# A list scheduler's table of priority offsets: 170 groups of operations in place of 21

## The chip, the cores and the metric

One core of one Trainium2 chip runs the whole program. The metric is device time in microseconds (us) of one execution; lower is better. Engines go by their names in the profile: PE is TensorE's matmul, PEld its weight load, DVE is VectorE, ACT is ScalarE, POOL is GpSimd, SP is SyncE, which issues all the DMAs here.

## The reference

Attention over 8 batches x 8 heads with queries averaged in pairs, and behind it a feed-forward block (FFN) whose gate is a cosine:

```python
q_pool = q.reshape(B, H, S // 2, 2, D).mean(axis=3)          # S 1152, D 64
scores = scale * q_pool @ k.transpose(0, 1, 3, 2)
attn = exp(scores - max(scores)); attn = attn / (sum(attn) + 1e-09)
x = (attn @ v).transpose(0, 2, 1, 3).reshape(B * S // 2, H * D)   # 4608 x 512
h = x @ w_in                                                   # 512 x 2048
out = (h * cos(h)) @ w_out                                     # 2048 x 512
```

All inputs and the output are f32; q and k have a spread of 0.8.

## The kernel before

To keep f32 accuracy with f16 matmuls, nearly each operand is split into a high and a low f16 part (cast on ACT, difference on POOL or DVE), and products are made as high x high, high x low, low x high.

Attention goes over 32 pairs of heads, each in 9 units. For a pair n, long before its units begin: K and q are loaded (SP), cast and split (`prep_k`, L745 and L746; `prep_q1`, L762; `prep_q2`, L775), and transposed by DMA into `k1`, `q1T`. PE makes trial scores into the banks `mx` (named m at L815, `mx_main`), DVE reduces them to row maxima `mxs` (L826), the maxima are negated into a column of `qs2`, which is transposed into `q2T`. In a unit: PE makes scores into two `st` banks (L1265; the rest rows L1286), ACT makes the exponent `e` (L1315) and its f16 cast `pp` (L1323), POOL or DVE the low part of `pp` (L1329, L1325), and PE multiplies with `vc`, V scaled, into the sums `ava` and `avb` (L1355; the mixed rows L1400), one PSUM bank each. For the first three pairs, and partly for the next ones, e is used as f32 (`NF32`, forms f32 of L1355 and L1400). At a pair's end `av_end` empties the two banks through DVE (L1454, L1459, L1462, L1469) into `xp`, of which there are two.

FFN goes over 18 chunks of 256 rows. A batch's four `xp` are scaled, split (`xs2`, L1523 ACT, L1525 DVE) and transposed to `xT`. `ffn1` multiplies with the two parts of w_in into banks `f` (L1630); ACT evicts each bank twice (L1654, L1657), DVE once (L1658); a sine (L1563), a product (L1569), a cast and a split (L1580, L1581) give the gate `g`; `ffn2` multiplies with w_out (L1690), DVE scales (L1734) and SP stores. The weights arrive as 64-bit floats: 16 pieces of 1 MB go through `big` buffers, DVE decodes each in three steps (L568, L571, L574; output named w for w_in and wf for w_out) and takes maxima (L585; for w_in ACT does, L581), ACT scales and casts (L608, L609), POOL splits (L612). w1 is ready when the last scale of w_in is there (L652 runs then). Until there is an FFN group to run, PE has attention alone. Sixty small warm-up matmuls (L663) stand between 14 and 26 us.

The order of the instructions on each engine is not that of the code. The code emits all instructions once; `arrange` then makes a list of 8,337 entries (one for each instruction of DVE, ACT, POOL and SP, one for a run of matmuls into one tile on PE), finds what depends on what, and schedules the list with estimated costs: each engine, when it comes free, takes of the entries that are ready the one with the smallest key. A key is the entry's place in the code's order plus an offset. The result is then fixed: each engine runs its instructions strictly in that order, with the usual semaphore waits. The offset comes from the table `SHIFT`, looked up by engine, operation, tiles written and tiles read:

```python
if nd["ins"][0].name in fill:
    off += len(nodes)
elif group in SHIFT:
    off += SHIFT[group][k * 1 // len(nodes)]
nd["key"] = (k + off, k)
```

A negative offset lets a group go ahead of others that are ready at the same time, a positive one lets it stand back. Tiles in the table go by the tag of their buffer: mx is the trial scores' banks, f those of FFN, `big` the large buffers (raw weights, FFN's h and y), `w2_1` also the place where w_in is decoded, `w2_0` that where pair 1's q and k lie at first.

Of the kernel before, what the change touches and what calls it, by code (L numbers as in the profile page):

```python
# [62 lines left out]
HS = (-16, -15, -14, -13, -12, -10, -12, -11, -10, -9, -8, -7, -7)  # L63

SHIFT = {
    ("Activation", "Activati", "big", "big"): (20,),
    ("Activation", "Activati", "big", "big/wsc"): (80,),
    ("Activation", "Activati", "vc_0", "sv/vld"): (20,),
    ("Activation", "TensorCo", "pp", "e"): (-80,),
    ("DVE", "TensorRe", "wmx", "big"): (-20,),  # L70
    ("DVE", "TensorSc", "big", "big/f/r1a"): (-40,),
    ("DVE", "TensorSc", "vc_1", "sv/vc_1/vld"): (80,),
    ("DVE", "TensorTe", "big", "big"): (20,),
    ("DVE", "TensorTe", "xp", "ava/rs"): (-300,),
    ("DVE", "TensorTe", "xp", "avb/rs"): (-40,),
    ("PE", "Matmult", "avb", "g/w2_0/w2_1"): (20,),
    ("PE", "Matmult", "avb", "w1_0/w1_1/xT"): (-20,),
    ("PE", "Matmult", "mx", "k1_0/q1T"): (-150,),
    ("PE", "Matmult", "mx", "w1_0/w1_1/xT"): (-40,),
    ("PE", "Matmult", "st", "g/w2_0/w2_1"): (-150,),  # L80
    ("PE", "Matmult", "st", "k1_1/k2_0/q1T/q2T"): (-20,),
    ("Pool", "TensorTe", "w2_1", "big/w2_0"): (-150,),
    ("SP", "DMACopy", "out_0", "xo"): (-150,),
    ("SP", "DmaTrans", "k1_0", "kst"): (-20,),
    ("SP", "DmaTrans", "q1T", "q1s"): (20,),
    ("SP", "DmaTrans", "xT", "xs2"): (150,),
}
# [1882 lines left out]
```

## Time and profile before

| | us |
|---|---|
| median of 3 runs | 1528.41 |
| lowest, highest | 1524.58, 1537.75 |
| the profiled execution's own time | 1523.91 |
| its span, first to last instruction | 1522.1 |
| PE busy in it | 1489.3 (98%) |
| ACT, DVE, POOL busy | 1231.5, 1042.9, 978.7 |

The rows below come from the profiled execution. Its own time is the one to set beside its span; the median of the runs is what a change is measured by. The share of busy time is an average over stretches with different limits, so a row for a stretch says more than one for the whole.

### The profile page before, as it was taken

To read this page: it belongs to the slowest core of one execution; us is meant where nothing else is said; L and a number is where in the kernel's file an instruction comes from. 1 tells how busy PE (TensorE), PEld (TensorE's weight loads), DVE (VectorE), ACT (ScalarE), POOL (GpSimd) and SP (SyncE) were. 2 spreads that over 40 slices of the span, in tenths; PEclk is the share of its full clock that TensorE was granted. 3 is DMA by queue.
4 is the path that set the end of the run, shared out by engine and by line. 5 is a ranking of instruction groups with operands and counts; after the bars stand their busy time and mean duration, and the time that the engine had idled before them with its cause. 6 is when DMAs were issued, how large, how long until landed. Compare 5 with 4: busy or idle time off the path is not lost.

```text
span 1522.1 us, 37816 instructions
## 1 busy us (share of the span) xinstructions
PE 1489.3 (98%) x15569; PEld 1022.5 (67%) x15569; DVE 1042.9 (69%) x1935; ACT 1231.5 (81%) x1925; POOL 978.7 (64%) x852
## 2 busy tenths in 40 slices
PE   6999899999999999999999999999999999999998
PEld 4777677667666576666666667666666667766665
DVE  6998876856786687786747776766777775532332
ACT  5778689998999799997977897998998898944442
POOL 4454567886776868778575676686878677531222
PEclk9999999999999999999999999999999999999999
DMA  9976634534255343535322425345352521001000
GB/s 257 299 211 150 172 82 96 116 76 108 71 102 111 98 91 73 127 68 138 83 73 65 98 63 115 78 99 104 87 108 73 110 56 31 11 27 30 20 17 22
DMA packets 226110, 145.07 MB, mean 95 GB/s; under 512 B 202448, under 2 KB 204752, under 8 KB 223888
## 3 DMA queue, kind: packets, MB, share of 16 engines
q1 hardware_dynamic: 225936, 142.65, 39.8%
q8 instruction: 122, 2.00, 0.5%
q14 instruction: 52, 0.43, 0.1%
HBM read 74.45 MB, written 10.49 MB: 56 GB/s over the span
## 4 chain that ended last, share of the span: by engine, by line
PE 84%; DVE 6%; ACT 5%; DMA 2%; issue 1%; POOL 1%; SPq 0%; ACTq 0%; DVEq 0%; POOLq 0%
PE f L1630 20%; PE f L1690 19%; PE st L1265 14%; PE ava L1355 8%; PE avb L1355 6%; PE m L815 6%; PE st L1286 2%; DVE mxs L826 2%; PE mx L1690 1%; DMA kld<-in_k_dram 1%; ACT e L1315 1%; PE ava L1400 1%; ACT pp L1323 1%; PE st L1630 1%; PE mx L856 1%
## 5 line engine op out<-in xcount | busy, mean ns | idle before, releaser
L1329 POOL TENSOR_TENSOR pp<-e,pp 128x512 f16<-128x512 f32 x438 | 531.0, 1236 | 235.7 <-ACT pp L1323 121.2
L826 DVE TENSOR_REDUCE mxs<-m 128x1 f32<-128x512 f32 x464 | 304.0, 681 | 109.9 <-PE m L815 108.1
L1630 PEld LDWEIGHTS <-w 128*128 128x128 f16 x3456 | 333.2, 98 | 65.6 <-DVE y L1658 2.1
L1630 PE MATMUL f<-xT,w 128*128 128x256 f16 x3048 | 365.6, 273 | 2.1 <-DVE y L1658 2.1
L1315 ACT ACTIVATE e<-st 128x512 f32<-128x512 f32 x534 | 295.8, 604 | 48.6 <-PE st L1265 26.7
L1690 PE MATMUL f<-w,g 128*128 128x512 f16 x1440 | 333.3, 379 | 0.0
L1581 POOL TENSOR_TENSOR g<-hsc,g 128x512 f16<-128x512 f32 x144 | 185.9, 1312 | 172.3 <-ACT g L1580 136.9
L1323 ACT CAST pp<-e 128x1024 f16<-128x1024 f32 x267 | 282.0, 1056 | 4.7 <-PE avb L1355 2.1
L1690 PEld LDWEIGHTS <-g 128*128 128x128 f16 x1680 | 161.1, 98 | 182.5 <-issue 0.7
L1355 PEld LDWEIGHTS <-pp 128*128 128x128 f16 (+1 forms) x5857 | 236.6, 100 | 67.5 <-issue 12.8
L1265 PE MATMUL st<-q1T,k 128*128 128x512 f16 x576 | 218.7, 380 | 2.6 <-ACT pp L1315 1.6
L1265 PE MATMUL st<-q2T,k 128*128 128x512 f16 x576 | 218.7, 380 | 0.0
L1355 PE MATMUL ava<-vc,pp 128*128 128x65 f16 (+6 forms) x4020 | 214.6, 202 | 2.3 <-DVE lx L1485 1.5
L1355 PE MATMUL avb<-vc,pp 128*128 128x65 f16 (+3 forms) x2329 | 176.8, 207 | 0.3 <-POOL pp L1329 0.3
L1265 PEld LDWEIGHTS <-k 128*128 128x128 f16 x1152 | 100.8, 98 | 95.1 <-issue 20.4
L1569 DVE TENSOR_TENSOR hsc<-hsc,y 128x512 f32<-128x512 f32 x144 | 133.8, 962 | 40.4 <-ACT y L1563 40.1
L815 PE MATMUL m<-k,q1T 128*128 128x512 f16 x464 | 154.6, 380 | 4.8 <-DVE mxs L826 4.1
L1658 DVE SCALAR_TENSOR_TENSOR y<-f,r1a,y 128x512 f32<-128x512 f32 x127 | 94.6, 746 | 81.6 <-ACT y L1657 79.4
L1654 ACT ACTIVATE hsc<-f,small 128x512 f32<-128x512 f32 x127 | 88.4, 696 | 62.7 <-PE f L1630 62.3
L1580 ACT CAST g<-hsc 128x512 f16<-128x512 f32 x144 | 88.7, 626 | 30.6 <-PE f L1690 29.6
L1325 DVE TENSOR_TENSOR pp<-e,pp 128x1024 f16<-128x1024 f32 x48 | 84.8, 1767 | 31.1 <-ACT pp L1323 22.8
L746 POOL TENSOR_TENSOR kst<-kld,kst 128x1152 f16<-128x1152 f32 x30 | 72.6, 2420 | 28.6 <-ACT kst L745 18.4
(183 smaller groups left out, 1898.5 us busy)
## 6 DMA issues: line engine op xcount, KB each, us to landing
vld<-in_v_dram SPq DMA_DIRECT2D x32, 576.0 KB, 3.9
...
```

Of the source, the lines that this page charges most:

```text
L815: nc.tensor.matmul(banks[h], q1T[n][:, h * QT + t, :], kmain(n, k1[n % 3], c, h), start=True, stop=True, skip_group_check=True,),
L826: nc.vector.reduce_max(mxs[n][:, h * QT + t, c : c + 1], banks[h], axis=AX.X)
L1265: nc.tensor.matmul(s[y].rearrange("p (t c) -> p t c", c=P), kcol(p, w, j, h), x[:, h * QT : (h + 1) * QT, :], start=part == 0, stop=part == 1,
L1315: nc.scalar.activation(e[:, c], b[:, 0 : c.stop - c.start], AF.Exp, scale=exp_scale, bias=l_add)
L1323: nc.scalar.copy(pp[:, 0, c0:n], e[:, c0:n])
L1329: nc.gpsimd.tensor_sub(pp[:, 1, c], e[:, c], pp[:, 0, c])
L1355: mm = nc.tensor.matmul(out, w, x, start=start, stop=False, skip_group_check=True)
L1569: nc.vector.tensor_mul(hj, hj, y[:, j : j + 2])
L1581: nc.gpsimd.tensor_sub(gt[:, 1], hj, gt[:, 0])
L1630: mm = nc.tensor.matmul(ps[:, fi, :], w1[wt][:, hp, fs], ck.xT[hp][:, xi, cs], start=n == 0, stop=n == 3 * HP - 1, skip_group_check=True,)
L1658: nc.vector.scalar_tensor_tensor(yj, ps, ra, yj.bitcast(I32), ALU.mult, ALU.subtract)
L1690: nc.tensor.matmul(po, gt[:, gi, f % 2, ts_], w2[wt][:, f, :], start=f == 0 and (gi, wt) == (0, 0), stop=f == NF - 1 and (gi, wt) == (1, 0),)
```

## The change

Only the table `SHIFT` is changed. It had 21 groups with offsets between -300 and 150; it has 170 groups now, of the 190 that the list has, with offsets between -600 and 600 in steps of 5. Each group of both tables occurs in the kernel. No instruction, tile, buffer or dependency is touched, nor the costs that the scheduler goes by; what changes is the order on the five engines. Lines of groups that the prediction doesn't speak of are left out of the diff.

```diff
 SHIFT = {
-    ("Activation", "Activati", "big", "big"): (20,),
-    ("Activation", "Activati", "big", "big/wsc"): (80,),
-    ("Activation", "TensorCo", "pp", "e"): (-80,),
-    ("DVE", "TensorSc", "big", "big/f/r1a"): (-40,),
-    ("DVE", "TensorTe", "big", "big"): (20,),
-    ("DVE", "TensorTe", "xp", "ava/rs"): (-300,),
-    ("DVE", "TensorTe", "xp", "avb/rs"): (-40,),
-    ("PE", "Matmult", "mx", "k1_0/q1T"): (-150,),
-    ("PE", "Matmult", "st", "k1_1/k2_0/q1T/q2T"): (-20,),
-    ("Pool", "TensorTe", "w2_1", "big/w2_0"): (-150,),
-    ("SP", "DMACopy", "out_0", "xo"): (-150,),
-    ("SP", "DmaTrans", "q1T", "q1s"): (20,),
-    ("SP", "DmaTrans", "xT", "xs2"): (150,),
...
+    ("Activation", "Activati", "big", "big"): (-110,),
+    ("Activation", "Activati", "big", "big/wsc"): (435,),
+    ("Activation", "Activati", "big", "f/r1a"): (-600,),
+    ("Activation", "Activati", "big", "f/small"): (-585,),
...
+    ("Activation", "Activati", "e", "st"): (285,),
...
+    ("Activation", "Activati", "pp", "st"): (-600,),
...
+    ("Activation", "Activati", "w2_1", "w2_1/wsc"): (-290,),
...
+    ("Activation", "TensorCo", "kst", "kld"): (585,),
+    ("Activation", "TensorCo", "pp", "e"): (-340,),
...
+    ("Activation", "TensorCo", "q1s", "qld"): (430,),
...
+    ("Activation", "TensorCo", "w1_0", "w2_1"): (-600,),
+    ("Activation", "TensorCo", "w2_0", "big"): (-170,),
...
+    ("DVE", "TensorRe", "mxs", "f"): (145,),
+    ("DVE", "TensorRe", "mxs", "mx"): (180,),
+    ("DVE", "TensorRe", "mxs", "st"): (-215,),
...
+    ("DVE", "TensorRe", "wmx", "big"): (35,),
...
+    ("DVE", "TensorSc", "big", "big"): (520,),
+    ("DVE", "TensorSc", "big", "big/f/r1a"): (185,),
...
+    ("DVE", "TensorSc", "w2_1", "big"): (430,),
+    ("DVE", "TensorSc", "w2_1", "big/w2_1"): (120,),
...
+    ("DVE", "TensorSc", "xs2", "ratio/xp/xs2"): (-600,),
+    ("DVE", "TensorTe", "big", "big"): (235,),
...
+    ("DVE", "TensorTe", "pp", "e/pp"): (380,),
...
+    ("DVE", "TensorTe", "xp", "ava/rs"): (-80,),
+    ("DVE", "TensorTe", "xp", "avb/rs"): (545,),
...
+    ("PE", "Matmult", "f", "ident/wmx"): (-440,),
...
+    ("PE", "Matmult", "mx", "k1_0/q1T"): (-340,),
...
+    ("PE", "Matmult", "mx", "k1_2/k2_0/q1T/q2T"): (-585,),
...
+    ("PE", "Matmult", "st", "k1_1/k2_0/q1T/q2T"): (-420,),
...
+    ("Pool", "TensorTe", "g", "big/g"): (10,),
+    ("Pool", "TensorTe", "kst", "kld/kst"): (-85,),
+    ("Pool", "TensorTe", "pp", "e/pp"): (-215,),
+    ("Pool", "TensorTe", "pp", "pp"): (-600,),
+    ("Pool", "TensorTe", "pps", "es/pps"): (-600,),
...
+    ("Pool", "TensorTe", "qs2", "q1s/qld"): (-375,),
+    ("Pool", "TensorTe", "w1_1", "w1_0/w2_1"): (-185,),
...
+    ("Pool", "TensorTe", "w2_1", "big/w2_0"): (-200,),
+    ("SP", "DMACopy", "big", "in_moe_w_in"): (245,),
+    ("SP", "DMACopy", "big", "in_moe_w_out"): (435,),
...
+    ("SP", "DMACopy", "kld", "in_k"): (-560,),
+    ("SP", "DMACopy", "out_0", "xo"): (365,),
...
+    ("SP", "DmaTrans", "q1T", "q1s"): (65,),
...
 }
```

## Rows read from the trace of the kernel before

**Rows 1.** Page, part 1: each engine's busy time.
```profile
...
PE 1489.3 (98%) x15569; PEld 1022.5 (67%) x15569; DVE 1042.9 (69%) x1935; ACT 1231.5 (81%) x1925; POOL 978.7 (64%) x852
...
```

**Rows 2.** Five stretches from start: columns in the first line.
```profile
...
core 0: us, PE busy (x) PEld busy (x) DVE busy (x) ACT busy (x) POOL busy (x), PEclk, DMA share, GB/s
...
12.00:228.00 216.00, 204.66 (x1887) 154.41 (x1888) 189.68 (x369) 160.03 (x266) 112.52 (x115) 0.99 0.74 193
228.00:1292.00 1064.00, 1058.44 (x11954) 714.24 (x11953) 767.58 (x1431) 951.82 (x1485) 786.87 (x666) 1.00 0.40 90
1292.00:1518.00 226.00, 226.00 (x1731) 153.85 (x1729) 81.02 (x130) 115.04 (x169) 69.11 (x56) 1.00 0.07 21
1518.00:1523.00 5.00, 0.19 (x2) 0.00 (x0) 0.42 (x1) 0.00 (x0) 0.00 (x0) 0.89 0.11 26
...
```

**Rows 3.** All waits of PE, longest first.
```profile
...
PE m L971 <- DMA q1T<-q1s: 12.1, 1, 12.1
PE m L815 <- DVE mxs L826: 4.1, 10, 1.1
...
```

**Rows 4.** Matmul groups from 12 to 228 us.
```profile
...
L1265 PE MATMUL st<-q2T,k 128*128 128x512 f16 x103 | 39.5, 383 | 0.0
...
L1400 PE MATMUL ava<-vc,pp 128*128 128x65 f32 x216 | 26.2, 273 | 0.0
...
L815 PE MATMUL m<-k,q1T 128*128 128x512 f16 x71 | 24.6, 386 | 3.6 <-DVE mxs L826 3.0 <-DVE amx L886 0.4
L1355 PE MATMUL ava<-vc,pp 128*128 128x65 f32 x144 | 18.7, 273 | 0.0
...
L1630 PE MATMUL f<-xT,w 128*128 128x256 f16 x132 | 15.9, 273 | 0.0
L901 PE MATMUL m<-k,q1T 128*128 128x512 f16 x32 | 10.5, 378 | 0.8 <-DVE mxs L916 0.7
...
L1022 PE MATMUL m<-k,q1T 128*128 128x128 f16 x2 | 0.3, 216 | 0.0
```

**Rows 5.** The chain's pieces, packed work: start, us, what.
```profile
...
70.06 1.79 PE ava L1400 x16
...
192.43 1.31 PE f L1630 x12
...
254.06 2.62 PE f L1630 x24
...
269.07 2.59 PE f L1690 x12
...
```

**Rows 6.** DVE groups from 12 to 228 us.
```profile
...
L826 DVE TENSOR_REDUCE mxs<-m 128x1 f32<-128x512 f32 x71 | 46.5, 680 | 12.1 <-PE m L815 12.0
...
L574 DVE SCALAR_TENSOR_TENSOR wf<-wraw,wf 128x1024 uint32<-128x1024 uint32 x8 | 11.1, 1392 | 0.0
L571 DVE SCALAR_TENSOR_TENSOR wf<-wraw,wf 128x1024 uint32<-128x1024 uint32 x8 | 10.7, 1332 | 0.0
...
L585 DVE TENSOR_REDUCE wmx<-wf 128x1 bf16<-128x1024 f32 x8 | 9.6, 1208 | 0.0
...
L568 DVE TENSOR_SCALAR wf<-wraw 128x1024 uint32<-128x1024 uint32 x8 | 6.3, 801 | 0.0
...
```

**Rows 7.** The chain's pieces in the first 15 us.
```profile
...
10.53 1.10 DVE w L568
...
14.14 0.61 DVE mxs L986
...
```

**Rows 8.** DVE's timeline from 118 to 120 us.
```profile
...
119.43 0.15 DVE L652 RECIPROCAL rw<-small 128x1 f32<-128x1 f32 x1
...
```

**Rows 9.** DVE's timeline from 776 to 822 us.
```profile
...
779.68 0.16 DVE L1454 TENSOR_SCALAR rs<-avb 128x4 f32<-128x4 f32 x1
...
818.64 0.41 DVE L1462 TENSOR_TENSOR xp<-avb,rs 128x256 f32<-128x256 f32 x1
...
```

**Rows 10.** The stretch between those two; columns as in rows 2.
```profile
...
784.00:820.00 36.00, 36.00 (x232) 22.01 (x230) 18.14 (x27) 23.71 (x38) 15.28 (x11) 1.00 0.22 56
...
```

More of the change, by code (lines that the diff above doesn't have):

```diff
@@ new lines @@
+    ("DVE", "TensorRe", "small", "p2w"): (395,),
+    ("DVE", "TensorRe", "small", "small"): (530,),
+    ("DVE", "TensorRe", "wmw", "f"): (-450,),
+    ("DVE", "TensorRe", "wmx", "big"): (35,),
+    ("DVE", "TensorSc", "amx", "amx"): (-265,),
+    ("DVE", "TensorSc", "big", "avb/big/r1a"): (-40,),
+    ("DVE", "TensorSc", "big", "big"): (520,),
+    ("DVE", "TensorSc", "big", "big/f/r1a"): (185,),
+    ("DVE", "TensorSc", "big", "big/mx/r1a"): (235,),
+    ("DVE", "TensorSc", "big", "big/r1a/st"): (-255,),
@@ new lines @@
+    ("DVE", "TensorSc", "es", "ava/rs"): (440,),
+    ("DVE", "TensorSc", "p2w", "wmw"): (-205,),
+    ("DVE", "TensorSc", "r1a", "small"): (-200,),
+    ("DVE", "TensorSc", "rs", "ava"): (-235,),
+    ("DVE", "TensorSc", "rs", "avb"): (220,),
+    ("DVE", "TensorSc", "small", "amx"): (-210,),
+    ("DVE", "TensorSc", "small", "fst"): (230,),
+    ("DVE", "TensorSc", "small", "p2w/rw"): (95,),
+    ("DVE", "TensorSc", "sv", "sv"): (130,),
+    ("DVE", "TensorSc", "vc_0", "sv/vc_0/vld"): (415,),
@@ new lines @@
+    ("DVE", "TensorSc", "vc_1", "sv/vc_1/vld"): (-320,),
+    ("DVE", "TensorSc", "w2_1", "big"): (430,),
+    ("DVE", "TensorSc", "w2_1", "big/w2_1"): (120,),
+    ("DVE", "TensorSc", "wmw", "wmw"): (40,),
+    ("DVE", "TensorSc", "xp", "ava/rs/xp"): (20,),
+    ("DVE", "TensorSc", "xp", "avb/rs/xp"): (-50,),
+    ("DVE", "TensorSc", "xs2", "ratio/xo/xs2"): (460,),
+    ("DVE", "TensorSc", "xs2", "ratio/xp/xs2"): (-600,),
+    ("DVE", "TensorTe", "big", "big"): (235,),
+    ("DVE", "TensorTe", "fst", "small"): (100,),
@@ new lines @@
+    ("DVE", "TensorTe", "kst", "kld/kst"): (-80,),
+    ("DVE", "TensorTe", "pp", "e/pp"): (380,),
+    ("DVE", "TensorTe", "qld", "qld"): (130,),
+    ("DVE", "TensorTe", "xo", "ava/osc"): (5,),
+    ("DVE", "TensorTe", "xo", "avb/osc"): (80,),
+    ("DVE", "TensorTe", "xo", "f/osc"): (-280,),
+    ("DVE", "TensorTe", "xo", "mx/osc"): (350,),
+    ("DVE", "TensorTe", "xo", "osc/st"): (560,),
+    ("DVE", "TensorTe", "xp", "ava/rs"): (-80,),
+    ("DVE", "TensorTe", "xp", "avb/rs"): (545,),
+    ("PE", "Matmult", "ava", "g/w2_0/w2_1"): (-5,),
@@ new lines @@
+    ("PE", "Matmult", "ava", "pp/pps/vc_0"): (-370,),
+    ("PE", "Matmult", "ava", "pp/pps/vc_1"): (20,),
+    ("PE", "Matmult", "ava", "pp/vc_0"): (20,),
+    ("PE", "Matmult", "ava", "pps/vc_0"): (-240,),
+    ("PE", "Matmult", "ava", "pps/vc_1"): (-145,),
+    ("PE", "Matmult", "ava", "w1_0/w1_1/xT"): (-65,),
+    ("PE", "Matmult", "ava/mx", "k1_0/pp/pps/q1T/vc"): (595,),
+    ("PE", "Matmult", "ava/mx", "k1_0/pps/q1T/vc_0"): (-20,),
+    ("PE", "Matmult", "ava/mx", "k1_1/pps/q1T/vc_0"): (-35,),
@@ new lines @@
+    ("PE", "Matmult", "ava/mx", "k1_1/pps/q1T/vc_1"): (-240,),
+    ("PE", "Matmult", "ava/mx", "k1_2/pps/q1T/vc_0"): (10,),
+    ("PE", "Matmult", "avb", "g/w2_0/w2_1"): (-20,),
+    ("PE", "Matmult", "avb", "pp/vc_0"): (-10,),
+    ("PE", "Matmult", "avb", "pp/vc_1"): (25,),
+    ("PE", "Matmult", "avb", "w1_0/w1_1/xT"): (-100,),
+    ("PE", "Matmult", "f", "ident/mxa"): (45,),
+    ("PE", "Matmult", "f", "ident/wmx"): (-440,),
+    ("PE", "Matmult", "f", "k1_0/k2_0/q1T/q2T"): (10,),
+    ("PE", "Matmult", "f", "k1_0/k2_1/q1T/q2T"): (300,),
@@ new lines @@
+    ("PE", "Matmult", "f", "k1_0/q1T"): (335,),
+    ("PE", "Matmult", "f", "k1_1/k2_1/q1T/q2T"): (-90,),
+    ("PE", "Matmult", "f", "k1_1/q1T"): (-40,),
+    ("PE", "Matmult", "f", "k1_2/k2_0/q1T/q2T"): (-320,),
+    ("PE", "Matmult", "mx", "g/w2_0/w2_1"): (5,),
+    ("PE", "Matmult", "mx", "ident/mxa"): (-10,),
+    ("PE", "Matmult", "mx", "k1_0/k2_0/q1T/q2T"): (-340,),
+    ("PE", "Matmult", "mx", "k1_0/k2_1/q1T/q2T"): (20,),
+    ("PE", "Matmult", "mx", "k1_0/q1T"): (-340,),
+    ("PE", "Matmult", "mx", "k1_1/k2_0/q1T/q2T"): (-450,),
@@ new lines @@
+    ("PE", "Matmult", "mx", "k1_1/k2_1/q1T/q2T"): (-225,),
+    ("PE", "Matmult", "mx", "k1_1/q1T"): (-55,),
+    ("PE", "Matmult", "mx", "k1_2/k2_0/q1T/q2T"): (-585,),
+    ("PE", "Matmult", "mx", "k1_2/k2_1/q1T/q2T"): (5,),
+    ("PE", "Matmult", "mx", "w1_0/w1_1/xT"): (-65,),
+    ("PE", "Matmult", "st", "g/w2_0/w2_1"): (-40,),
+    ("PE", "Matmult", "st", "k1_0/k2_0/q1T/q2T"): (-5,),
+    ("PE", "Matmult", "st", "k1_0/k2_1/q1T/q2T"): (-25,),
+    ("PE", "Matmult", "st", "k1_0/q1T"): (20,),
@@ new lines @@
+    ("PE", "Matmult", "st", "k1_1/k2_0/q1T/q2T"): (-420,),
+    ("PE", "Matmult", "st", "k1_1/k2_1/q1T/q2T"): (-35,),
+    ("PE", "Matmult", "st", "k1_2/k2_0/q1T/q2T"): (-20,),
+    ("Pool", "Memset", "k2_0", ""): (80,),
+    ("Pool", "Memset", "k2_1", ""): (-325,),
+    ("Pool", "Memset", "q1s", ""): (-410,),
+    ("Pool", "Memset", "qs2", ""): (-30,),
+    ("Pool", "Memset", "vc_0", ""): (535,),
+    ("Pool", "Memset", "vc_1", ""): (295,),
+    ("Pool", "Memset", "w2_0", ""): (70,),
+    ("Pool", "Memset", "xo", ""): (195,),
@@ new lines @@
+    ("SP", "DMACopy", "out_0", "xo"): (365,),
+    ("SP", "DMACopy", "qld", "in_q"): (15,),
+    ("SP", "DMACopy", "vld", "in_v"): (80,),
+    ("SP", "DMACopy", "w2_0", "in_k"): (20,),
+    ("SP", "DMACopy", "w2_0", "in_q"): (115,),
+    ("SP", "DMACopy", "xo", "left"): (430,),
+    ("SP", "DmaTrans", "k1_0", "kst"): (-85,),
+    ("SP", "DmaTrans", "k1_1", "kst"): (115,),
+    ("SP", "DmaTrans", "k1_1", "w2_0"): (215,),
+    ("SP", "DmaTrans", "k1_2", "kst"): (5,),
+    ("SP", "DmaTrans", "q1T", "q1s"): (65,),
@@ L87 @@
+    ("SP", "DmaTrans", "q2T", "qs2"): (10,),
+    ("SP", "DmaTrans", "q2T", "w2_0"): (-535,),
 }
```

49 lines of the change are left out of this document (41 added, 8 removed).

## The prediction

> **What bounds the kernel now.** I read the engines' busy times first, then the same by stretches, then what PE waits for, then the groups and the chain in the one stretch where PE is not full. TensorE (PE) is busy 1489.3 of 1522.1 us, 98%; ScalarE comes next with 81% [rows 1]. The 33 us that PE sits idle lie at few places [rows 2, 3]: 12.1 us before its first matmul, which waits for the transposed q of pair 0; 216.00 - 204.66 = 11.3 us from 12 to 228 us; 1064.00 - 1058.44 = 5.6 us in the long middle from 228 to 1292 us; none from 1292 to 1518 us, where only FFN is left; and some 3.9 us behind the last matmul, for the last scaling and its store. The granted clock is 1.00 nearly throughout, so TensorE runs at its 2.4 GHz level and its work has one price.
>
> Busy time flatters, since the records overlap: a 512-column matmul is shown as about 383 ns long [rows 4], while twelve in a row take 2.59 us, 216 ns each [rows 5]. So I count what the stretch from 12 to 228 us must cost: 2 x 103 score matmuls of L1265 at 216 ns (44.5 us), 2 x 216 of L1400 at 1.79/16 = 112 ns (48.4 us), 71 of L815 at 216 ns (15.3 us), 144 and 136 f32 ones of L1355 at 112 ns (31.4 us), 132 of L1630 at 1.31/12 = 109 ns (14.4 us) [rows 4, 5]. The 30 groups that follow, from L901 to L1022 and without the 60 warm-up matmuls, come to about 34.5 us by the same time for a column (256 columns in 109 ns) and at least 30 ns a piece, an estimate. Together 188.5 us in the 215.9 us after the first matmul: 27.4 us are lost there, 11.3 shown as idle, the rest hidden behind record ends and warm-up matmuls. The Trainium skill says the same of busy time (Trainium Kernel Development and Optimization, Performance Expectations: matmul busy time is a bad metric because matmuls are pipelined); the 383 against 216 ns bear it out. By busy time alone 11 us could be won in that stretch, by the count 27.
>
> Why there and nowhere else: until 192.43 us no FFN matmul exists [rows 5], because FFN needs the outputs of the first four pairs. Later, whenever attention is late, PE takes FFN groups. The best proof: pair 18's sums of avb are read at 779.68 us, its bank is emptied at 818.64 us [rows 9], 39 us without any place for the next pair's products, and PE is busy 36.00 of 36.00 us between [rows 10]. In the early stretch DVE is nearly as full as PE, 189.68 of 216 us [rows 2], and the two wait for each other: DVE for L815's scores 12.0 us [rows 6], PE for DVE's reductions of them 3.0 us shown [rows 4], of 4.1 us in the whole run [rows 3].
>
> **The change, part by part.** No instruction is added or removed, so all durations stay; only the place of each in its engine's queue moves. The list has 8,337 entries, 5.5 for each us of the span, 6.0 in the early part (the first FFN group is entry 1154 and runs at 192 us). An offset of 600 is thus at most some 100 to 110 us, two and a half pairs, and it acts only where two entries are ready at once on one engine.
>
> *Weights on DVE, in the early stretch.* The decode of w_out moves by +520 (entries 634 to 1166 become 1154 to 1686), the first step of that of w_in by +430, its other steps by +120, their loads on SP by +435 and +245. The w_out decode with its maxima (the wf groups) takes 11.1 + 10.7 + 9.6 + 6.3 = 37.7 us of DVE before 228 us [rows 6]; behind entry 1154 it stands after 192 us. DVE's load there falls from 189.7 to about 152 us, under PE's 188.5, and reductions of 0.68 us no longer stand behind decode steps of 0.8 to 1.4 us. Were DVE the whole cause, the 27.4 us less 3.4 of warm-up matmuls (60 at 56 ns, an estimate from the width) would go: 24 us. Against it: the reductions move too (mx +180, f +145), Pool's split of w_in comes ahead (-185), and list scheduling still starts a decode when nothing else is ready. Nearest row for what the present order costs visibly: PE's waits of L815 for DVE, 3.0 us in this stretch [rows 4]. Between 0 and 24 I take a third, 8 us.
>
> *The head.* The w_in load at +245 goes behind the first pair's loads. Now DVE starts the first decode at 10.53 us and reaches its first reduction at 14.14 us [rows 7], though PE's first matmuls came at 12.10 us; about 1.5 us of that is delay, since a reduction could start half a us after the matmul. The copies of q and k on ScalarE (+430, +585) have nothing ready against them that early: nothing. The first q1T transposition (+65) waits for its input alone: nothing. Between -2 and +2, I take -1 us.
>
> *The middle, 228 to 1292 us.* ScalarE: the FFN evictions to the front (-585, -600), exp of the scores back (+285), q and k copies back (+430, +585). DVE: the multiply that empties avb back by +545, FFN products back by +185 to +235, xs2 to the front (-600). Pool: its subtractions forward (-215, -375, -600). PE: score and maxima groups of some buffer numbers forward by up to 585. SP: K loads forward (-560), output stores back (+365), so K loads no longer stand behind a store that waits for its scaling. Cost on PE: 5.6 us of idle now, so between -5 and the price of whatever loses its FFN cover; with the cover of [rows 9, 10], zero. If that cover were gone, a hold of the avb bank of some us in each of 28 pairs would show fully.
>
> *The tail* is FFN alone at full rate; its order changes nothing. Sum: -8 - 1 + 0 = -9 us on the profiled execution, 1523.9 to 1515 us. That execution lies 4.5 us under the median of the three runs, 1528.4, so the median should come to 1519 us. What ends last stays PE.
>
> **The rivals.** (a) *Nothing moves.* The early stretch is held by the chain load, cast, split, transpose, scores, reductions, second transpose, not by order; then the 27.4 us stay and the time is 1524 to 1531. For: PE's shown wait of L815 for DVE, 3.0 us [rows 4], is a ninth of the loss. Against: DVE at 88% is too full to be innocent. (b) *The early stretch nearly closes.* Decode leaves DVE and it brings the full 24 us, less 2 to 8 for what a fixed chain keeps, and 2 in the middle: 1500 to 1512. Against: the floor would be met almost exactly. (c) *Slower: w_out comes too late.* Its decode at entries up to 1686, plus ScalarE's scaling (+435), puts the end of w_out's split near 192 + 532/5.5 = 289 us and 10 more, while the first product with it runs at 269.07 us now [rows 5]. Until then FFN has only the first halves of two chunks, 2 x 192 matmuls at 109 ns = 42 us for more than 100 us of time; `big` and `g` buffers then stand full and PE has attention alone, which leaves it unfilled as from 12 to 228 us, 27.4 / 216 = 13% of the time. For 30 us of delay that is 4 us, which the gain covers; it decides above some 150 us of delay, or if attention too comes to stand behind the late copies of q and k, at three times that loss: 12 to 30 us, 1540 to 1558. For: offsets that large are new on both sides, and w_in's scales, ready at 119.43 us [rows 8], lose their 70 us of lead as well. Against: the split needs 8 scalings and 32 Pool steps only, and Pool's go to the front.
>
> A rule of the Trainium skill speaks against moving Pool's work forward (SBUF — State Buffer, Who interferes with whom: DVE and GpSimd share a port pair as an exclusive lock, and the second of two such operations blocks). No row here separates such a block from other waits; Pool is busy 64% [rows 1], and a block of it would only matter where FFN cover is missing, so it stays inside rival (c).
>
> **How the numbers follow.** My forecast, a gain of 3 to 15 us on the median: 0.50, at 1519 us. (a) 0.16. (b) 0.18. (c) 0.16. A measurement of this kernel tells changes of about 1%, 15 us; the three runs alone lie within 13 us. Faster by over 1% is under 1513: (b) and a little of the forecast, 0.21. Slower by over 1% is above 1544: most of (c), 0.14. Within 1%: 0.65. The range leaves out the far half of (b) and nearly all of (c): 1505 to 1540 us. The unknown costs (0 to 24 in the early stretch, -2 to +2 in the head, -5 upward in the middle) lie within it but for the last.
>
> **What would show it.** In the profile after: PE's idle from 12 to 228 us under 11.3 us and the first L1630 before 192 us (the w_out step right); wf groups of DVE after 192 us rather than before; the first reduction near 13 us (the head); idle from 228 to 1292 us still around 5 us (the cover). Wrong would be: idle PE between 230 and 330 us with L1690 waiting for w2, which is (c); or the early stretch as now although decode has left it, which is (a) and would mean that DVE's fullness was no cause.

## The result, and the profile after

After: 1540.39 us (median of 20 runs), before beside it 1525.49 us; ratio 1.0083, 95% interval 1.0063 to 1.0104. Two of the 40 runs, one of each kernel (3527 us before, 1723 us after), lie far off all others and are left out of the ratio. By the ratio the table makes the kernel slower by some 13 us (the two medians lie 14.9 apart), where a gain of 9 was forecast. 1540.39 lies just above the range's upper end. The profiled execution has its own time of 1541.29 and a span of 1538.9 us, 16.8 above that of before. In the new file every line of the kernel is 149 higher: L815 is L964, L826 is L975, L1265 is L1414, L1315 is L1464.

First the engines' busy times of the kernel after, which answer to [rows 1]:

```profile
...
PE 1494.7 (97%) x15569; PEld 1026.0 (67%) x15569; DVE 1024.1 (67%) x1935; ACT 1236.6 (80%) x1927; POOL 977.4 (64%) x852
...
```

The counts are the same but for lost records, and so is the work. The stretches, as in [rows 2]:

```profile
...
12.00:228.00 216.00, 197.25 (x1792) 149.10 (x1793) 181.33 (x351) 147.71 (x249) 107.64 (x104) 0.96 0.76 191
228.00:1292.00 1064.00, 1054.53 (x11788) 709.73 (x11786) 741.89 (x1423) 950.65 (x1470) 777.97 (x664) 1.00 0.39 89
1292.00:1518.00 226.00, 225.91 (x1868) 155.08 (x1867) 95.23 (x156) 133.62 (x202) 81.91 (x67) 1.00 0.09 23
1518.00:1539.00 21.00, 16.96 (x127) 12.13 (x124) 1.54 (x3) 0.00 (x0) 0.82 (x1) 0.99 0.10 25
...
```

From 12 to 228 us PE runs 95 matmuls fewer than before, is idle 18.8 us in place of 11.3, and its granted clock is 0.96; in the long middle it is idle 9.5 us in place of 5.6. The tail is as full as before, only longer. The early stretch in four, of the kernel before:

```profile
...
12.00:38.00 26.00, 23.41 (x164) 15.41 (x165) 22.02 (x40) 14.42 (x25) 6.09 (x6) 1.00 1.05 267
38.00:128.00 90.00, 85.19 (x769) 63.72 (x769) 83.33 (x168) 67.04 (x116) 47.57 (x45) 0.99 0.85 235
128.00:190.00 62.00, 58.11 (x570) 44.78 (x569) 54.61 (x103) 45.24 (x76) 34.62 (x39) 0.99 0.69 170
190.00:228.00 38.00, 37.95 (x391) 30.50 (x391) 29.72 (x61) 33.34 (x53) 24.24 (x27) 1.00 0.34 82
...
```

and of the kernel after:

```profile
...
12.00:38.00 26.00, 19.37 (x118) 12.09 (x119) 19.68 (x35) 10.94 (x19) 5.91 (x5) 0.85 0.87 223
38.00:128.00 90.00, 87.18 (x799) 67.34 (x797) 80.47 (x154) 64.76 (x109) 45.39 (x43) 0.99 0.86 228
128.00:190.00 62.00, 52.71 (x477) 38.99 (x473) 53.25 (x107) 43.10 (x74) 33.40 (x35) 0.94 0.80 187
190.00:228.00 38.00, 38.00 (x407) 30.67 (x406) 27.92 (x57) 28.91 (x48) 22.95 (x23) 1.00 0.36 88
...
```

Two places lose in these two executions: the head up to 38 us (46 matmuls fewer, clock 0.85) and 128 to 190 us (93 fewer, clock 0.94). What PE waits for, in the whole run [rows 3]:

```profile
...
PE m L1120 <- DMA q1T<-q1s: 12.7, 1, 12.7
PE st L1414 <- ACT pp L1464: 7.5, 7, 2.1
PE mx L983 <- DVE mxs L975: 3.4, 4, 2.0
PE m L964 <- DVE mxs L975: 3.0, 9, 1.1
PE m L664 <- ACT vc L1280: 2.3, 1, 2.3
...
```

Scores wait seven times, 7.5 us in all, for an st bank that ScalarE has not read yet; before it was twice, 1.6 us. New is one wait for V. They are few, but each is up to 2.3 us long.

*The head.* PE's timeline (start, duration, what; in brackets the idle time before it and what ended it):

```profile
...
19.61 0.23 PE L664 MATMUL m<-ident,mxa 128*128 128x128 bf16 x1 [2.34 <-ACT vc L1280]
...
33.05 0.38 PE L1414 MATMUL st<-q1T,k 128*128 128x512 f16 x1 [2.14 <-ACT pp L1464]
...
```

At 19.61 the spread of V's maximum over the partitions stands in PE's queue ahead of trial scores that could run; it waits for ScalarE's pass over V, and that for V's load. At 33.05 the scores wait for an exponent. ScalarE's timeline says why it is late:

```profile
...
32.31 0.23 ACT L1188 ACTIVATE qs<-m 128x5 f16<-128x5 f32 x1 [2.04 <-DVE m L1187]
32.42 0.58 ACT L1464 ACTIVATE pp<-st 128x512 f32<-128x512 f32 x1
...
```

The copy of the maxima (offset -600) stands ahead of an exponent whose scores are there, and waits 2.04 us for DVE's m. The exponent's group (pp from st) has -600 too, so these two offsets don't set which goes first. DVE's timeline:

```profile
...
27.98 1.28 DVE L717 TENSOR_SCALAR w<-wraw 128x1024 uint32<-128x1024 uint32 x1
...
30.98 1.21 DVE L720 SCALAR_TENSOR_TENSOR w<-wraw,w 128x1024 uint32<-128x1024 uint32 x1
32.12 0.15 DVE L1187 TENSOR_REDUCE m<-mxs 128x5 f32<-128x15 f32 x1
...
```

Two decode steps of w_in run before the maxima are put together. So one step held on DVE holds ScalarE, and that holds PE: each engine takes its queue strictly in order.

*128 to 190 us.* ScalarE's timeline at its worst place:

```profile
...
173.85 1.55 ACT L911 CAST q1s<-qld 128x1024 f16<-128x1024 f32 x3 [0.96 <-POOL qld L900]
176.56 1.15 ACT L894 CAST kst<-kld 128x1152 f16<-128x1152 f32 x1 [1.16 <-DMA k<-kst]
...
177.92 1.16 ACT L1280 ACTIVATE vc<-vld 128x1152 bf16<-128x1152 f32 x1
...
179.08 1.06 ACT L1464 ACTIVATE pp<-st 128x512 f32<-128x512 f32 x2
...
```

The q and K casts of a later pair, put back by +430 and +585, still stand ahead of two exponents (pp from st, -600); they wait 0.96 and 1.16 us for their own inputs, and PE's scores at 179.70 us wait 1.96 us for the exponents. PE's timeline has that wait:

```profile
...
179.70 0.38 PE L1414 MATMUL st<-q1T,k 128*128 128x512 f16 x1 [1.96 <-ACT pp L1464]
...
```

At 143 us it is DVE. A step of xs2 (offset -600) takes 1.69 us ahead of a reduction, and PE's trial scores wait 1.99 us. First DVE's timeline, then PE's:

```profile
...
143.26 1.69 DVE L1674 SCALAR_TENSOR_TENSOR xs<-xp,ratio,xs 128x512 f16<-128x512 f32 x1
144.87 0.68 DVE L975 TENSOR_REDUCE mxs<-m 128x1 f32<-128x512 f32 x1
...
145.60 0.55 PE L983 MATMUL mx<-k,q1T 128*128 128x128 f16 x7 [1.99 <-DVE mxs L975]
...
```

*Decode of w_out* did not leave. DVE's groups of the kernel after from 12 to 228 us, for [rows 6]:

```profile
...
L975 DVE TENSOR_REDUCE mxs<-m 128x1 f32<-128x512 f32 x64 | 41.9, 681 | 6.8 <-PE m L964 6.7
L723 DVE SCALAR_TENSOR_TENSOR wf<-wraw,wf 128x1024 uint32<-128x1024 uint32 x8 | 11.6, 1456 | 0.0
L720 DVE SCALAR_TENSOR_TENSOR wf<-wraw,wf 128x1024 uint32<-128x1024 uint32 x8 | 10.7, 1342 | 0.0
...
L734 DVE TENSOR_REDUCE wmx<-wf 128x1 bf16<-128x1024 f32 x8 | 9.7, 1210 | 0.0
...
L717 DVE TENSOR_SCALAR wf<-wraw 128x1024 uint32<-128x1024 uint32 x8 | 6.9, 885 | 0.0
...
```

All eight pieces are still decoded there; the last decode step begins at 195.4 us (before 195.9). The first FFN product starts at 194.43 us (before 192.43), the first with w_out at 278.8 (before 269.07), w1 is ready at 120.43 (before 119.43).

To compare kernels by stretch I set each matmul at its time in an unbroken row, as the prediction did, and subtract the work started from the time gone. The work is 1456 us in every kernel; what is left is the loss, whether it shows as idle time, as a lower clock or not at all. The last column is the mean time per run at the lower of the clock's two levels, 1.2 GHz: twice the span times (1 - mean clock), over each kernel's runs.

| kernel | ratio to before, 95% | lost to 38 us | 38 to 190 | 190 to 1292 | us at 1.2 GHz |
|---|---|---|---|---|---|
| before | 1 | 22.7 | 16.5 | 22.2 | 4 to 9 |
| after | 1.0083 [1.0063, 1.0104] | 29.3 | 21.2 | 27.4 | 18.5 |
| e1_new_early | 1.0010 [0.9984, 1.0036] | 27.6 | 14.4 | 21.3 | 10.0 |
| e2_new_late | 1.0006 [0.9981, 1.0031] | 22.1 | 17.2 | 27.3 | 5.1 |
| e3_weights_old | 1.0320 [1.0283, 1.0358] | 32.2 | 41.9 | 35.9 | 62.0 |
| e4_head_old | 1.0064 [1.0039, 1.0090] | 21.4 | 29.8 | 28.9 | 26.4 |
| e5_v_behind | 1.0007 [0.9987, 1.0028] | 23.4 | 15.4 | 28.5 | 4.6 |
| e6_late_exp_old | 1.0116 [1.0086, 1.0146] | 21.9 | 17.5 | 42.6 | 11.8 |
| e7_warm | 1.0099 [1.0068, 1.0129] | 27.8 | 22.5 | 26.9 | 12.8 |
| e8_before_warm | 1.0035 [1.0011, 1.0059] | 22.5 | 21.6 | 23.0 | 13.8 |
| e9_moved | 1.0093 [1.0065, 1.0121] | 28.5 | 21.9 | 27.9 | 16.4 |
| j_after_1 | 1.0089 [1.0057, 1.0121] | 29.9 | 13.3 | 33.1 | 11.3 |
| j_after_2 | 1.0117 [1.0086, 1.0148] | 30.2 | 13.4 | 34.4 | 21.6 |
| j_before_1 | 1.0011 [0.9986, 1.0036] | 23.9 | 17.4 | 16.8 | 18.6 |
| f1_late_act | 1.0003 [0.9983, 1.0022] | 21.4 | 15.9 | 27.4 | 9.2 |
| f2_late_dve | 0.9967 [0.9939, 0.9994] | 22.3 | 23.0 | 21.4 | 7.9 |
| f3_late_rest | 0.9970 [0.9951, 0.9989] | 21.9 | 22.1 | 21.8 | 3.4 |
| f4_v_behind_old_late | 0.9976 [0.9950, 1.0001] | 23.8 | 15.6 | 23.0 | 2.1 |
| g1_act_old | 1.0006 [0.9984, 1.0029] | 28.3 | 12.6 | 26.2 | 10.7 |
| g2_late_no_act | 0.9984 [0.9961, 1.0006] | 21.9 | 15.4 | 22.5 | 5.8 |

The losses are of one profiled execution each, the ratios of all. Of the 16.8 us between the two profiled spans 6.6 lie before 38 us, 4.7 up to 190, 5.2 in the middle.

How far one execution can be trusted shows in kernels that share an order. By tile names and shapes in the traces, e2, f1, f2, f3 and g2 have the order of before on PE, DVE, ScalarE and Pool up to 192 us. Their losses to 38 us lie between 21.4 and 22.7, from 38 to 190 us between 15.4 and 23.0. So the 6.6 us of the head are clear of this spread, the 4.7 us between 38 and 190 are not. For that stretch the waits are the better sign: e9, which has after's order but for four moves, waits there for the same things as long (3.4 us for DVE's maxima, 3.2 for exponents; after 3.4 and 4.0).

### The profile page after: what moved, and what is told of

Its sections match the earlier page's. It is cut to its first block, busy times and chain, and to the rows that moved or that the text cites. A ratio compares the mean times of both kernels' runs of the same rounds, so it can differ in the third digit from the quotient of the medians.

```text
span 1538.9 us, 37866 instructions
## 1 busy us (share of the span) xinstructions
PE 1494.7 (97%) x15569; PEld 1026.0 (67%) x15569; DVE 1024.1 (67%) x1935; ACT 1236.6 (80%) x1927; POOL 977.4 (64%) x852
## 4 chain that ended last, share of the span: by engine, by line
PE 81%; ACT 9%; DVE 5%; DMA 3%; issue 1%; POOL 1%; SPq 0%; ACTq 0%; DVEq 0%; POOLq 0%
PE f L1779 19%; PE f L1839 18%; PE st L1414 14%; PE ava L1504 8%; PE avb L1504 5%; PE m L964 5%; PE st L1435 1%; ACT e L1464 1%; PE mx L1839 1%; DMA k<-kst 1%; ACT pp L1472 1%; PE ava L1549 1%; DVE mxs L975 1%; DMA wraw<-in_moe_w_in_dram 1%; ACT y L1712 1%
## 5 line engine op out<-in xcount | busy, mean ns | idle before, releaser
L975 DVE TENSOR_REDUCE mxs<-m 128x1 f32<-128x512 f32 x464 | 303.0, 682 | 77.2 <-PE m L964 75.7
L1464 ACT ACTIVATE e<-st 128x512 f32<-128x512 f32 x534 | 301.3, 601 | 52.5 <-POOL pp L1478 27.4
L1839 PE MATMUL f<-w,g 128*128 128x512 f16 x1440 | 332.9, 379 | 0.0
L1504 PEld LDWEIGHTS <-pp 128*128 128x128 f16 (+1 forms) x5857 | 240.9, 100 | 88.4 <-issue 21.3
L1472 ACT CAST pp<-e 128x1024 f16<-128x1024 f32 x267 | 280.4, 1050 | 18.9 <-PE avb L1504 11.8
L1839 PEld LDWEIGHTS <-g 128*128 128x128 f16 x1680 | 158.5, 98 | 175.2 <-issue 1.4
L1414 PE MATMUL st<-q1T,k 128*128 128x512 f16 x576 | 219.2, 381 | 9.2 <-ACT pp L1464 7.5
L1414 PE MATMUL st<-q2T,k 128*128 128x512 f16 x576 | 219.1, 380 | 0.0
L1504 PE MATMUL ava<-vc,pp 128*128 128x65 f16 (+6 forms) x4020 | 194.8, 202 | 2.5 <-DVE lx L1634 1.9
L1414 PEld LDWEIGHTS <-k 128*128 128x128 f16 x1152 | 104.2, 98 | 100.5 <-issue 23.1
L1718 DVE TENSOR_TENSOR hsc<-hsc,y 128x512 f32<-128x512 f32 x144 | 128.7, 929 | 46.4 <-ACT y L1712 46.3
L1504 PE MATMUL avb<-vc,pp 128*128 128x65 f16 (+3 forms) x2329 | 158.7, 207 | 0.8 <-DVE sv L1296 0.4
L964 PE MATMUL m<-k,q1T 128*128 128x512 f16 x464 | 154.4, 379 | 5.1 <-DVE mxs L975 3.0
L1474 DVE TENSOR_TENSOR pp<-e,pp 128x1024 f16<-128x1024 f32 x48 | 74.6, 1554 | 24.4 <-ACT pp L1472 12.9
```

Of the source, the lines that this page charges most:

```text
L964: nc.tensor.matmul(banks[h], q1T[n][:, h * QT + t, :], kmain(n, k1[n % 3], c, h), start=True, stop=True, skip_group_check=True,),
L975: nc.vector.reduce_max(mxs[n][:, h * QT + t, c : c + 1], banks[h], axis=AX.X)
L1414: nc.tensor.matmul(s[y].rearrange("p (t c) -> p t c", c=P), kcol(p, w, j, h), x[:, h * QT : (h + 1) * QT, :], start=part == 0, stop=part == 1,
L1464: nc.scalar.activation(e[:, c], b[:, 0 : c.stop - c.start], AF.Exp, scale=exp_scale, bias=l_add)
L1472: nc.scalar.copy(pp[:, 0, c0:n], e[:, c0:n])
L1504: mm = nc.tensor.matmul(out, w, x, start=start, stop=False, skip_group_check=True)
```

## The experiments

Letters of theories in the quoted expectations hold within one group of runs. In code, `k` is the entry's place in the list of 8,337, `OLD` the table of before; 1154 is the first FFN entry, at 192 us. Where nothing else is said, a kernel is the one after with the edit shown.

**Which half of the list.** New offsets for early entries alone, and for late ones alone:

```diff
-        elif group in SHIFT:
-            off += SHIFT[group][k * 1 // len(nodes)]
+        else:
+            off += (SHIFT if k < 1154 else OLD).get(group, (0,))[0]    # e1
+            off += (OLD if k < 1154 else SHIFT).get(group, (0,))[0]    # e2
```

> The new table for the first 1154 entries of the list (all that the code emits before the first FFN group, some 190 us), the old table for the rest. Theory A (most of the loss is made in the early stretch, where PE has no FFN work to fall back on): 9 to 13 us slower than before, about 1535 to 1538 us, with PE idle and a halved clock at 20 to 35 us as in the changed kernel. Theory B (the loss is the late stretches', where emptying ava and avb comes late): within 3 us of before, about 1525 us.

> The old table for the first 1154 entries, the new one for the rest. Theory A: 3 to 6 us slower than before, about 1528 to 1531 us, with the first 190 us as before. Theory B: 12 to 16 us slower, about 1538 us.

1530.48 and 1528.66 us: neither half costs anything that its interval tells from nothing, while both together cost 0.83%. That is against Theory B, and A's price for the early half doesn't show. In the loss columns e1 has the head of the kernel after (27.6) and the middle of before, e2 the reverse.

e1 says more than that. By tile names and shapes its order is the one of after on PE up to PE's 1,291st matmul (176 us in after, 172 in e1), on DVE and ScalarE up to 174 us of after. So it carries the head's waits (1.70 us for V, 1.18 for an exponent, a loss of 27.6) and the 2.0 us wait for DVE's maxima behind the step of xs2, and its ratio is still 1.0010. Its profiled execution from 128 to 190 us:

```profile
...
128.00:190.00 62.00, 57.15 (x546) 43.09 (x545) 54.66 (x105) 48.01 (x84) 36.88 (x39) 1.00 0.78 187
...
```

So, by the ratios, 0.73 of the 0.83% come with the order behind 174 us, and with e2 beside it the new late offsets cost this only behind the new early ones.

**The weights.** Old offsets for the 17 groups that load, decode, scale and split the weights:

```diff
+WEIGHTS = [("Activation", "Activati", "big", "big/wsc"), ("DVE", "TensorSc", "big", "big"),
...
+for g in WEIGHTS:
+    SHIFT[g] = OLD.get(g, (0,))
```

> The new table, but the 17 groups of the weights' preparation (decode, maxima, scaling, cast, split, loads) have their old offsets. If the weights' steps on DVE and ScalarE are what PE's score banks wait for at 128 to 180 us: 1531 to 1535 us. If they are innocent: 1540 us as the changed kernel.

1578.32 us, 3.2% slower, which neither theory had. With the rest of the table as it is, the weights' new offsets save time: without them V's spread waits 7.4 us in the head and PE's clock is 0.88 from 12 to 228 us.

**The head.** Old table for the first 194 entries:

```diff
+            off += (OLD if k < 194 else SHIFT).get(group, (0,))[0]
```

> The old table for the first 194 entries (pair 0's preparation and the warm-up matmuls, some 30 us), the new one for the rest. If the wait of PE and DVE for V's maximum at 17 to 20 us, with the halved clock behind it, makes the 6 to 7 us that are lost by 38 us: 1532 to 1535 us, no clock below 1.00 before 38 us. If the later early stretch gives it back as waiting: 1538 to 1541 us.

1540.87 us. The windows of e4:

```profile
...
12.00:38.00 26.00, 23.82 (x172) 15.66 (x171) 21.97 (x41) 14.74 (x25) 8.12 (x6) 1.00 1.08 261
38.00:128.00 90.00, 81.65 (x633) 61.46 (x631) 73.19 (x134) 55.23 (x94) 37.94 (x37) 0.83 0.79 213
128.00:190.00 62.00, 59.25 (x581) 46.25 (x581) 57.21 (x118) 49.19 (x84) 35.14 (x41) 1.00 0.75 189
...
```

The head is even better than before (172 matmuls to 164), and the next stretch loses it all and more: 633 matmuls to 769, clock 0.83. From 128 to 190 us less is lost than before (581 matmuls to 570), though ScalarE's new offsets hold there. Both places are repaired in this execution, and the kernel is no faster by more than the intervals tell.

Next, the spread of V's maximum put behind the first trial scores of the second head, as a dependency that the scheduler sees:

```diff
+        if (h, t) == (1, 0):
+            after(v_spread[0], mm)
```

> The new table, with one more order of two matmuls of PE: the spread of V's maximum (pair 0) may come only after the first trial score of the second head. If PE and DVE, each in its fixed order, lose their time by 38 us to that wait for V (2.3 us on PE, then late reductions): PE's wait for V's maximum at 17 to 20 us under 1 us, and the median 3 to 5 us under the changed kernel, 1535 to 1537 us. If the loss moves to the next wait: within 2 us of 1540 us.

1527.6 us, level with before: 12 us won, by the ratios 0.76 of the 0.83%, which is more than either theory had. All offsets of the new table are kept here, ScalarE's too. But this edit makes a new list; only 55 to 60% of the instructions of PE, DVE and ACT stand at the same place as after. So e9 keeps the order of the kernel after and moves only four instructions by hand on PE and DVE, those trial scores and reductions, ahead of V's spread and its reduction:

```diff
+    for name, ahead in moves:
+        row = order[nodes[node_of[name]["eng"]]]
...
+                row.insert(row.index(k), j)
```

> The changed kernel's order, kept instruction for instruction, but for four moves by hand: two trial-score matmuls of pair 0 on PE and their two reductions on DVE come ahead of the steps that wait for V's maximum. Theory H (the wait itself, and the lateness that follows it in the same order, makes most of the loss): 1533 to 1536 us, with 4 to 6 us less lost by 38 us. Theory D (the 12 us that the earlier kernel with V's spread held back won came mostly from the rest of the list being scheduled anew): 1538 to 1540 us.

1538.87 us: the theory that this one wait starts the loss fell. PE's timeline of e9:

```profile
...
28.37 0.38 PE L1428 MATMUL st<-q2T,k 128*128 128x512 f16 x1 [1.04 <-DMA q2T<-qs]
...
32.91 0.61 PE L1060 MATMUL m<-k,q1T 128*128 128x512 f16 x2 [1.92 <-DMA q1T<-q1s]
33.35 0.97 PE L1563 MATMUL ava<-vc,pp 128*128 128x65 f32 x6
...
```

The wait for V is down to 0.7 us, and PE now stands 1.92 us at pair 1's trial scores, for their transposed q, with AV products (L1563) behind them in its queue. The loss to 38 us is 28.5 where it was 29.3.

**One late group.** e2 with the late exponents' offset (+285) taken back to 0:

```diff
+            if k >= 1154 and group == ("Activation", "Activati", "e", "st"):
+                off -= 285
```

> As the kernel with the old table for 1154 entries and the new one behind them, but exp (e from st) at offset 0 in the late part instead of 285. If the exponents that stand behind FFN's evictions on ScalarE are what the middle loses: PE's waits of st for exp from 228 to 760 us fall from 3.5 to under 1.5 us, and the time by 2 to 3 us to about 1526 us. If it is the reductions or the emptying of ava and avb: no change, 1528 to 1530 us.

1543.76 us, 1% slower than e2, the reverse of what the offset's sign suggests and outside both theories. e6's windows show one place:

```profile
...
684.00:760.00 76.00, 66.76 (x853) 46.91 (x850) 55.67 (x115) 67.44 (x107) 52.40 (x47) 0.96 0.54 125
...
```

PE is idle 9.2 of 76 us there, 5.2 of it waiting for e; nothing like it is in e2 (0.8 us idle). FFN, which had covered such waits [rows 9, 10], does not cover them there; why, no run shows.

**The clock.** If the lower clock were the cause, more warm-up matmuls would help. The 60 become 190, until 52 us, in the kernel after (e7) and in before (e8):

```diff
-FILL = (14.0, 26.0, 0.2)
+FILL = (14.0, 52.0, 0.2)
```

> The new table, with 190 warm-up matmuls up to 52 us instead of 60 up to 26 us. If the halved clock at 20 to 40 us follows from PE's idle time there: the time at the halved clock falls from about 18 to under 12 us per execution, and the median by 2 to 4 us, to 1536 to 1538 us. If the clock falls without regard to it: 1539 to 1542 us.

> The old table with the same 190 warm-up matmuls. If part of the spread of the kernel before (1521 to 1538 us) is the halved clock in the first 60 us: less time at the halved clock, a median of 1522 to 1525 us. If not: as the kernel before.

1540.14 and 1530.87 us: no gain for after, a loss of 0.35% for before. In e7's profiled execution the clock falls all the same, at 38 and at 147 us, though its runs have 12.8 us at 1.2 GHz in place of 18.5. Since the added matmuls cost before something by themselves, e7 does not bound what the lower clock costs.

**Chance or table.** An offset of its own between -10 and 10 for each group, on top of the new table (two draws) and of the old one:

```diff
+        if nd["ins"][0].name not in fill:
+            off += zlib.crc32(repr((1, group)).encode()) % 21 - 10
```

> The new table with a random whole number between -10 and 10, fixed for each of the 190 groups, added to every offset (2 us of list at most). Theory C (on the chip either table is one draw among near-equal orders, which differ by a few waits that the scheduler's model does not see): somewhere between 1525 and 1545 us, not near 1540. Theory S (the table's own content costs the 0.8%): within 3 us of 1540 us.

> The new table with a second draw of random additions between -10 and 10. Theory C: again between 1525 and 1545 us, some us away from the first draw. Theory S: within 3 us of 1540 us.

> The old table with the same random additions. Theory C: between 1522 and 1545 us, likely above the kernel before, whose table is a chosen draw. Theory S: within 3 us of the kernel before.

1538.88, 1543.45 and 1527.29 us. Both draws on the new table keep the loss, the one on the old table has none. So the loss belongs to the table, not to a draw of this size. Where it falls differs, though: both j_after lose 8 us less than after between 38 and 190 us (of which execution alone can make most) and 6 to 7 more in the middle. The stretch from 128 to 190 us of j_after_1, with ScalarE's new offsets and the loss of the whole, is better than that of before:

```profile
...
128.00:190.00 62.00, 59.04 (x598) 46.05 (x598) 57.61 (x112) 47.46 (x82) 36.02 (x40) 1.00 0.82 183
...
```

j_before_1 also bears on the clock: 18.6 us per run at 1.2 GHz, as much as after, and a ratio of 1.0011.

**Which engine, late.** Old table, and for entries from 1154 on the new offsets of ScalarE alone, of VectorE alone, and of PE, Pool and SyncE:

```diff
+            off += (SHIFT if k >= 1154 and group[0] in ("Activation",) else OLD).get(group, (0,))[0]    # f1
+            off += (SHIFT if k >= 1154 and group[0] in ("DVE",) else OLD).get(group, (0,))[0]           # f2
+            off += (SHIFT if k >= 1154 and group[0] in ("PE", "Pool", "SP") else OLD).get(group, (0,))[0]    # f3
```

> The new offsets of ScalarE alone, and only for entries from 1154 on; everything else has the old table. The late part as a whole cost about 4.5 us at full clock (e2 against before), most of its extra waits of PE being scores st that wait for ScalarE's exp (3.5 against 0.5 us between 228 and 760 us). Theory A (the late exp at +285 behind FFN evictions at -585 to -600 is what costs): 1528 to 1531 us, 3 to 5 us above the kernel before, with waits of st for e of 3 us or more. Theory B (no one engine's groups cost anything by themselves, only their combination): within 2 us of the kernel before, st's waits for e under 1 us.

> The new offsets of VectorE alone, and only for entries from 1154 on. In e2 PE's maxima tiles m waited 4.0 us for VectorE's reductions between 228 and 760 us, 1.8 before. Theory A (ScalarE's groups are the cost): within 2 us of the kernel before, 1524 to 1527. Theory C (VectorE's are: reductions at +145 and +180, emptying of avb at +545): 1528 to 1531 us with waits of m for mxs of 3 us or more.

> The new offsets of PE, Pool and SyncE, and only for entries from 1154 on. Theories A and C both: within 2 us of the kernel before. Theory D (the order of PE's own groups, scores and maxima forward by up to 585, takes FFN's cover from later stretches): 1528 to 1533 us, with the loss between 228 and 760 us spread over several waits.

1527.97, 1524.05 and 1523.0 us, with before at 1528.62 beside them. No part by itself is slower than before; VectorE's and the rest's are 0.3% faster, more than any theory gave them. ScalarE's is 4 to 5 us above these two, though level with before. PE's waits for it from 228 to 760 us:

```profile
...
PE st L1438 <- ACT e L1488: 3.0, 1, 3.0
...
```

That is one wait; f3 has 0.4 us of this kind there, f2 and before none that the view lists. The quoted 3.5 us for e2 is 1.1 by this view. f1 also has the middle loss of the whole late part, 27.4 us, though two dips of the clock in its profiled execution, 6.8 us in all, take part in that. That pointed to ScalarE, weakly.

**ScalarE.** g1 is the kernel after with ScalarE's 36 groups on the old table throughout; g2 is before with all late offsets but ScalarE's:

```diff
+            off += (OLD if group[0] == "Activation" else SHIFT).get(group, (0,))[0]    # g1
+            off += (SHIFT if k >= 1154 and group[0] != "Activation" else OLD).get(group, (0,))[0]    # g2
```

> The new table but for ScalarE, whose 36 groups have their old offsets (four of the old table, 0 for the others) at every entry. Theory A (ScalarE's order carries the loss): 1524 to 1530 us, within 4 us of the kernel before, a loss at 38 us near 23 us as before and no waits of st for exp of over 1 us in the early stretch. Theory B (any mixture of offsets this large loses 5 to 15 us, whoever's): 1534 to 1545 us. The q spread and V's steps of VectorE keep their new offsets, so some of the head's loss may stay under A: then 1530 to 1533.

> Old table for entries below 1154; from there on the new one for VectorE, PE, Pool and SyncE, the old one for ScalarE. Theory A: as VectorE's part and the rest's alone (ratios 0.9967 and 0.997), 1519 to 1526 us, 2 to 7 us under the kernel before, with waits of st for e between 228 and 760 us under 1.5 us. Theory B: as the whole late part (ratio 1.0006) or above, 1528 to 1536 us.

g1: 1530.57 us, with before at 1529.38. Some 0.77 of the 0.83% go when ScalarE's offsets go. The windows of g1:

```profile
...
12.00:38.00 26.00, 19.86 (x123) 12.14 (x124) 20.32 (x36) 10.94 (x19) 5.89 (x5) 1.00 0.90 216
...
128.00:190.00 62.00, 59.35 (x577) 45.62 (x575) 56.05 (x105) 47.57 (x82) 34.27 (x41) 1.00 0.73 184
...
```

From 128 to 190 us PE runs 577 matmuls in place of 477, at clock 1.00, more than before (570). The waits of st for an exponent there, after and then g1:

```profile
...
PE st L1414 <- ACT pp L1464: 4.0, 3, 2.0
...
PE st L1438 <- ACT pp L1488: 0.8, 1, 0.8
...
```

The head is nearly as bad as after, 123 matmuls, with waits of 1.75 us for V (after 2.34) and the same 2.14 for an exponent: that part is not ScalarE's. g1's middle, 26.2 us, isn't mended either, against Theory A. g2: 1525.09 us, level with before; f2's and f3's small gains don't add up.

g1 does not make ScalarE the cause. e5, e1 and e2 take as much away (ratios 1.0007, 1.0010 and 1.0006), e5 with every one of ScalarE's new offsets kept. In single executions the stretch that g1 mends is also mended in e4 (581 matmuls), in j_after_1 (598) and in e5:

```profile
...
128.00:190.00 62.00, 58.83 (x578) 44.72 (x576) 58.38 (x98) 46.98 (x80) 36.66 (x39) 1.00 0.77 179
...
```

Two of these three, e4 and j_after_1, lose by their ratios all the same. And g1's edit makes a new list as well: ScalarE's own order leaves that of after at 56 us. What the runs show is that the loss needs the whole: several unlike edits each undo nearly all of it.

**The halves that lost least**, e5's early part and the old late part:

```diff
+            off += (SHIFT if k < 1154 else OLD).get(group, (0,))[0]    # on e5
```

> The new table for entries below 1154 with V's spread on PE held behind the first trial scores of the second head (as in e5), the old table for entries from 1154 on. If the losses of the two parts add, as they did within 2 us so far: e5 lost 67.9 us in its profiled run, 4 to 5 of it from the late part, so some 63 us, and a median of 1520 to 1525 us, level with the kernel before or up to 5 us faster. If a reshuffled list is a new draw each time, as e5 and e6 suggest, anything from 1520 to 1540.

1524.47 us, as the sum of the losses had it (62.4 us by the three columns, e5 67.3). f2, f3 and f4 are the best kernels here, some 4 to 5 us under before; that is a third of the 1% that a single measurement tells, and only the intervals of f2 and f3 stay below 1.

## Why the prediction was wrong

The sum was -8 for the decode of w_out, -1 for the head and 0 for all the rest. Measured are 13 us of loss. Two steps failed: the gain of 8 us was 0, and the waits that the new order brings were put at nothing, or at 2 us at most in the head. Which offsets make the loss behind the head stays open.

- **The w_out decode**, -8 us: the step that failed first. All eight pieces ran before 228 us still, 38.9 us of DVE in place of 37.7, and DVE's load from 12 to 228 us fell to 181.3 us, not to about 152. An offset acts only among entries that are ready at one time. The prediction named this against itself ("list scheduling still starts a decode when nothing else is ready") and then took a third of 24 us all the same; that DVE had nothing else ready is the likely reason, argued and not traced in the scheduler. The gain was 0. (g1, e1 and both j_after lose 2 to 4 us less than before from 38 to 190 us, within what executions of one order differ by.)
- **The head**, -2 to +2: DVE's first reduction came at 13.36 us, 0.8 sooner [rows 7], as reckoned, but the head lost 6.6 us. Only the w_in load, the q and K copies and one transposition were priced. V's spread, its reduction and ScalarE's pass over V were not looked at, nor decode steps in front of the maxima. That V's place in PE's order takes part is shown by f4 against e1: the same offsets but for V's spread held back, 23.8 us lost instead of 27.6. That moving it alone isn't enough is shown by e9. And the head alone is not the 13 us: e1 has it and a ratio of 1.0010.
- **ScalarE**, nothing: "the copies of q and k ... have nothing ready against them" was said of the head alone, and from 38 to 228 us ScalarE's order was not priced. From 173 to 179 us of after two of those casts, and at 126 and 128 us a copy of maxima and a scaling of the weights (waits of 1.35 and 1.44 us), stand ahead of exponents, before PE has FFN work. That these waits occur is shown; that ScalarE's offsets are the cause is not, since e5 loses nothing with all of them. The cover was named as the condition, then applied only to the middle.
- **The middle**, 0: it lost 5.2 us more in the profiled execution. Each kernel with ScalarE's new late offsets lost 26.9 us or more there, those without 16.8 to 23.0, but for g1 with 26.2. In e2 and f1 such a loss does not show in the ratio (1.0006 and 1.0003). What holds g1's middle is open. Which of ScalarE's late groups it might be is open too: taking one back (e6) gave a new place with 9 us of idle.
- **One price for a matmul.** The clock was taken to stay at 1.00 nearly throughout, as before. In after it was 0.85 in the head and 0.94 from 128 to 190 us; in g1 it was 1.00 in the head, with waits of 1.75 us for V and 2.14 for an exponent (after 2.34 and 2.14). A line through each kernel's runs, span against time at 1.2 GHz, gives 0.36 us for each such us in after and 0.6 to 0.8 in before; 11 us more of it (18.5 less 7.1) go with 4 to 9 of the 13 us. These slopes hold the stalls too, so they are no price of the clock by itself. By j_before_1, as much time at 1.2 GHz comes without a loss.
- **Rival (c)** had the sign and, at 1540 to 1558 us, just the time, but not the mechanism. Products with w_out began 10 us later, and from 228 to 304 us PE was idle 1.6 us, with no wait of L1839 for w2. Its side remark, attention behind the late copies of q and K, is seen at 173 to 179 us, but because those copies stand too early for their inputs, not too late.
- **Right**: PE ends last, and the tail is at full rate. Whether relief of DVE would have paid is not shown, since DVE was not relieved.
